# A recurrent attention with router and two feed-forward layers on one core: whole-chunk loads, products in halves, fillers in a bank of their own

## The chip, the core and the metric

The kernel runs on one core of a Trainium2 chip. The metric is the device time in microseconds (us) of one execution. Five engines work from queues of their own, each strictly in its written order: TensorE (PE, with its weight loads shown as PEld), VectorE (DVE), ScalarE (ACT), GpSimd (POOL) and SyncE (SP), which issues most transfers. They meet at semaphores.

## What is computed

The reference, cut to what matters. The shapes are B = 4, H = 8, S = 768, D = 48; N = 3072 tokens of 384 values; E = 8 experts with hidden width 1024; then a dense layer of width 2048.

```python
for t in range(S):                                   # recurrent attention, one state per (b, h)
    cur = np.einsum('bhd,bhe->bhde', u[None] * kt, vt)
    y[:, :, t] = np.einsum('bhd,bhde->bhe', rt, state + cur)
    state = wt[:, :, :, None] * state + np.einsum('bhd,bhe->bhde', kt, vt)
# the expert layer on x = y as (N, 384)
xn = x / (np.linalg.norm(x, axis=-1, keepdims=True) + 1e-06)
en = expert_emb / (np.linalg.norm(expert_emb, axis=-1, keepdims=True) + 1e-06)
logits = xn @ en.T / tau
expert_idx = np.argmax(logits, axis=1)               # each token goes to one expert
out[mask] = gate_w[mask, None] * (np.maximum(x[mask] @ w1[e], 0.0) @ w2[e])
# the dense layer
h = x @ w_in
out = (h * np.tanh(softplus(h))) @ w_out
```

## The kernel before

The program has three stages: the attention with the router woven into it, the expert layer, and the dense layer. The change touches the first alone, and that stage ends when the last token rows have been sent to their experts.

**Chunks.** The 768 steps are cut into NCH = 12 chunks of C = 64 steps. A chunk holds all 32 pairs of batch and head: two heads lie one above the other on the 128 partitions (48 rows used of each 64), 16 such pairs along the free axis. For each chunk, `load` and `load_v` bring w, r, k and v. Before, each comes in two transfers of 48 (v: 64) partitions, through `copy_in`, which views the rows as 12 (v: 8) groups. `scaled` makes running products of w from both ends with two VectorE scans (PRE, SUF) and from them RH = r·PRE (POOL) and KH = k·SUF (VectorE).

**Products on TensorE.** All are fp32, and the profile counts two records for one such product. For a chunk: `keys` (transposes of KH), `bonus` (RK = r·k from POOL as the weights, the columns of u as the moving side: the term of a step with itself), `dots` (KH by RH inside the chunk), `sums` (into the state) and `fn` in `outputs` (RH by the state, L617, then the matrix `at` by v, L622). The router handles two tiles of 128 tokens per chunk (`Router.tile`): `turn` (transposes of x), `logits` (x by the expert embeddings), then ScalarE copies; after 6, 6, 6, 4 and 2 tiles `decide` ranks the tokens of that group (norm by `inv_norm`, arg max, ranks on TensorE) and `send` scatters the tiles' rows to the table xs in DRAM by POOL's indirect transfers.

**The matrix `at`** is made of the bonus spread on a diagonal (h = 0 by eight ScalarE activations, L548; h = 1 by one POOL product, L558, as ON_POOL says for every chunk) and the dots copied into its upper part by VectorE (L565).

**Fillers.** Ahead of each chunk's bonus TensorE runs FILL = 2 bf16 products of 128x512 whose result nobody reads (L541); they write the PSUM bank that the bonus then uses. After the attention 60 more products of 128x256 (`ahead`, L981) follow.

**What sets the order.** The scheduler of the framework is off. Every step is registered with `plan.add`; the list ORDER names the steps in the order of issue, and BANKS names for each temporary result one of seven PSUM banks. An engine takes its own steps of that list in that order. Transfers issued by SP use eight completion semaphores in turn, so one waits for the eighth before it.

**At the end of the stage** the last scatter must land before SP loads the first expert's rows (`load_rows`, L957); ScalarE and VectorE scale them, TensorE turns them (L1007), and the first expert product (L1021) starts.

## Time and profile before

| what | us |
|---|---|
| median of 3 runs (lowest, highest) | 815.65 (815.36, 817.05) |
| the profiled execution, its own time | 821.62 |
| its span, first to last instruction | 819.9 |
| first work of TensorE | 11.9 |
| end of the last chunk's outputs on TensorE | 152.2 |
| first expert product | 179.25 |

The profile gives, for each engine, busy time by groups of instructions and by stretches of the span, the waits with the engine that ended them, and a timeline in which a row stands for consecutive instructions of one kind. A weight load and the product that uses it overlap, so a group's busy time divided by its count is a pace and not the length of one. The rows used are in a section of their own below.

### The profile page before, as it was taken

The numbers are of one execution on the slowest core, as the hardware profiler recorded it, in microseconds if no ns is written. First come the engines' busy times: TensorE is split into PE (matmuls) and PEld (weight loads), VectorE is DVE, ScalarE is ACT, GpSimd is POOL, SyncE is SP. The second block draws the span as 40 slices with busy tenths as digits, with TensorE's granted clock in tenths as the row PEclk, the third lists the DMA queues.
The fourth block names the chain that finished last, engine by engine and source line by source line (L and its number), as shares of the span: only waits on it lengthen the run. The fifth ranks groups of instructions, "written<-read, shape, count | busy, mean of one in ns | idle before, by whom it ended". The sixth has DMA issues, their size and how long they took to land. (4 is left out here: it accounts for less than half of the span.)

```text
span 819.9 us, 17379 instructions
## 1 busy us (share of the span) xinstructions
PE 777.7 (95%) x6464; PEld 715.9 (87%) x6464; DVE 638.3 (78%) x954; ACT 484.6 (59%) x1049; POOL 431.7 (53%) x391
## 2 busy tenths in 40 slices
PE   3998999789999999999999999999999999999995
PEld 3897987768999999989989999999999999999994
DVE  9895885558988898898878778877876776876773
ACT  4584665436566656647556566666656665665653
POOL 9695866337778787767433353334334334335331
PEclk9998899779999999999999999999999999999998
DMA  6765453167777777775200010000001001001001
GB/s 183 196 195 162 150 158 125 60 187 186 199 175 180 196 185 181 193 199 177 59 1 1 0 40 1 1 20 20 1 1 40 1 0 39 1 2 39 0 1 44
DMA packets 61357, 73.79 MB, mean 90 GB/s; under 512 B 8966, under 2 KB 51886, under 8 KB 61262
## 3 DMA queue, kind: packets, MB, share of 16 engines
q1 hardware_dynamic: 57422, 63.11, 28.4%
q0 software_dynamic: 3840, 9.47, 3.2%
q8 instruction: 53, 0.87, 0.5%
q14 instruction: 42, 0.34, 0.1%
HBM read 61.86 MB, written 10.69 MB: 88 GB/s over the span
## 5 line engine op out<-in xcount | busy, mean ns | idle before, releaser
L1151 POOL TENSOR_TENSOR t<-t,t 128x512 f32<-128x512 f32 x94 | 121.9, 1299 | 237.2 <-ACT t L1147 231.7
L1160 DVE TENSOR_TENSOR gl<-t,gh 128x512 fp32r<-128x512 f32 (+1 forms) x97 | 114.1, 1176 | 74.5 <-ACT gh L1157 74.2
L1144 ACT ACTIVATE t<-t,two 128x512 f32<-128x512 f32 (+1 forms) x97 | 69.9, 720 | 118.4 <-DVE t L1141 118.4
L872 PE MATMUL acc<-woh,gl 128*128 128x384 f32 x384 | 129.6, 338 | 0.1
L870 PE MATMUL acc<-woh,gh 128*128 128x384 f32 x384 | 129.3, 337 | 0.0
L871 PE MATMUL acc<-wol,gh 128*128 128x384 f32 x384 | 129.0, 336 | 0.0
L949 POOL TENSOR_TENSOR w0l<-r,w0h 128x384 fp32r<-128x384 f32 x63 | 68.4, 1086 | 60.2 <-ACT w0h L948 52.3
L865 PE MATMUL ph<-xl,wih 128*128 128x512 f32 x240 | 95.0, 396 | 0.0
L864 PE MATMUL ph<-xh,wil 128*128 128x512 f32 x240 | 94.8, 395 | 0.0
L863 PE MATMUL ph<-xh,wih 128*128 128x512 f32 x240 | 93.3, 389 | 0.0
L870 PEld LDWEIGHTS acc<-woh,gh 128*128 128x128 f32 x384 | 72.2, 188 | 4.2
L949 POOL TENSOR_TENSOR w1l<-r,w1h 128x384 fp32r<-128x384 f32 x63 | 74.6, 1184 | 1.9 <-ACT w1h L948 1.5
L871 PEld LDWEIGHTS acc<-wol,gh 128*128 128x128 f32 x384 | 72.1, 188 | 4.0
L872 PEld LDWEIGHTS acc<-woh,gl 128*128 128x128 f32 x384 | 72.0, 188 | 0.4 <-DVE gl L1160 0.4
L865 PE MATMUL acc<-hl,w1h 128*128 128x428 f32 (+7 forms) x192 | 67.2, 350 | 3.6 <-DVE hl L1030 3.4
L1154 DVE TENSOR_TENSOR t<-t,ph 128x512 f32<-128x512 f32 (+1 forms) x97 | 64.8, 668 | 5.8 <-POOL t L1151 5.7
L863 PE MATMUL acc<-hh,w1h 128*128 128x428 f32 (+7 forms) x192 | 67.6, 352 | 1.8 <-DVE yT L1045 1.8
L1157 ACT CAST gh<-t 128x512 fp32r<-128x512 f32 (+1 forms) x97 | 58.8, 606 | 16.5 <-DVE t L1154 14.3
L1141 DVE SCALAR_TENSOR_TENSOR t<-t 128x512 f32<-128x512 f32 (+1 forms) x97 | 66.2, 683 | 2.1 <-ACT t L1137 2.1
L1134 DVE TENSOR_SCALAR t<-ph 128x512 f32<-128x512 f32 (+1 forms) x97 | 65.3, 674 | 2.4 <-PE ph L865 2.2
L864 PE MATMUL acc<-hh,w1l 128*128 128x428 f32 (+7 forms) x192 | 66.1, 344 | 0.0
L863 PE MATMUL ph<-xh,w0h 128*128 128x420 f32 (+7 forms) x189 | 65.2, 345 | 0.0
(221 smaller groups left out, 1855.9 us busy)
## 6 DMA issues: line engine op xcount, KB each, us to landing
r<-in_moe_w SPq DMA_DIRECT2D x128, 192.0 KB
d<-in_moe_w_in SPq DMA_DIRECT2D x16, 384.0 KB
d<-in_moe_w_out SPq DMA_DIRECT2D x16, 384.0 KB
r<-in_r_t SPq DMA_DIRECT2D x24, 192.0 KB
k<-in_k_t SPq DMA_DIRECT2D x24, 192.0 KB
v<-in_v_t SPq DMA_DIRECT2D x24, 192.0 KB
w<-in_w_t SPq DMA_DIRECT2D x22, 198.0 KB
xs<-zs SPq DMA_DIRECT2D x1, 1203.1 KB
```

The lines of the kernel that those rows point to most:

```text
L863: mm(out, lhsT=wh, rhs=xh, start=start, stop=False)
L864: mm(out, lhsT=wl, rhs=xh, start=False, stop=False)
L865: mm(out, lhsT=wh, rhs=xl, start=False, stop=stop)
L870: mm(out, lhsT=ah, rhs=bh, start=start, stop=False)
L871: mm(out, lhsT=ah, rhs=bl, start=False, stop=False)
L872: mm(out, lhsT=al, rhs=bh, start=False, stop=stop)
L949: (eng or nc.gpsimd).tensor_tensor(lo, r, f32(hi), op=ALU.subtract)
L1134: nc.vector.tensor_scalar(tile_of(i, "t0", mt, bufs=3)[:, q], S[i]["ph"][:, q], 20.0, None, op0=ALU.min)
L1141: nc.vector.scalar_tensor_tensor(t0, t0, 2.0, t0, op0=ALU.add, op1=ALU.mult)
L1144: nc.scalar.activation(tile_of(i, "t1", mt)[:, q], S[i]["t0"][:, q], AF.Ln, bias=g.two)
L1151: (nc.gpsimd if i < TI - 2 else nc.vector).tensor_tensor(t0, t0, S[i]["t1"][:, q], op=ALU.mult)
L1160: nc.vector.tensor_tensor(tile_of(i, "gl", ghl, F32R)[:, q], S[i]["t0"][:, q], f32(S[i]["gh"][:, q]), op=ALU.subtract)
```

## The change

- **Loads.** The two heads' 48 rows now lie next to one another (partitions 16 to 111: LEAD = 16, HEADS), so w, r and k of a chunk come in one transfer of 96 partitions each; v in two of 64, without the view in groups. The first load of w keeps its 128 partitions. The initial rows of the table xs are written by eight transfers of 100 rows instead of one of 8 x 100.
- **Bonus and logits in halves.** Each product with 128 weight columns becomes two with 64, whose results go to the lower and the upper half of the PSUM partitions.
- **Fillers.** None ahead of the bonus any more; FILL = 37 single fillers (L637) are steps of their own, in the last PSUM bank, and six banks are left for BANKS.
- **`at`.** ON_POOL holds for even chunks alone; in the six odd ones ScalarE makes h = 1 as well.
- **Sums of squares.** In `decide`, VectorE first copies them to PSUM (`twin`), and the later product reads the copy.
- **u.** Its two small copies into `ub` go from VectorE to ScalarE.
- **A new ORDER and a new BANKS**, with changed costs in the planner's steps (bonus 0.9 + 0.44 becomes 1.7).

```diff
-FILL = 2
-ON_POOL = [(s, 1) for s in range(NCH)]
+FILL = 37
+ON_POOL = [(s, 1) for s in range(0, NCH, 2)]
...
 ORDER = [
-    2, 16, 18, 6, 3, 4, 10, 0, 20, 19, 27, 9, 8, 11, 5, 7, 31, 12, 17, 32, 25, 29, 37, 38,
+    2, 20, 27, 10, 18, 29, 0, 11, 3, 7, 6, 1, 8, 4, 16, 5, 19, 31, 32, 12, 154, 17, 109, 9,
...
+    if twin is not None:
+        add("dve", STEP, lambda: v.tensor_copy(s2, ss), [src], [ks])
...
-            ("dve", lambda: v.tensor_tensor(t, ss, r, op=ALU.mult), [src, kr], kt),
+            ("dve", lambda: v.tensor_tensor(t, s2, r, op=ALU.mult), [ks, kr], kt),
...
-                nc.tensor.matmul(lg(), lhsT=xT[:, c], rhs=g.enT[:, c], start=c == 0, stop=c == KC - 1)
+                for q in COLS:
+                    nc.tensor.matmul(lg()[q], lhsT=xT[:, c, q], rhs=g.enT[:, c], start=c == 0, stop=c == KC - 1)
...
-    def copy_in(x, rows, e=SPREAD):
-        b = rows.shape[0] // e
-        nc.sync.dma_start(x, rows.rearrange("(b e) n -> e b n", b=b))
...
+            q = HEADS if s else slice(0, 128)
+            add("sp", BW * 0.3, lambda: nc.sync.dma_start(W[s % NW][q], g.w_t[s, q]), [], [("w", s % NW)], wake=1.3)
...
-        for h in range(2):
-            out = dst[s % NR][64 * h:64 * h + D].rearrange("p n t -> p (n t)")
-            add("sp", BW * 0.2, lambda out=out, h=h: copy_in(out, src[s, h]), [], [(nm, s % NR)], wake=1.3)
+        add("sp", BW * 0.3, lambda: nc.sync.dma_start(dst[s % NR][HEADS].rearrange("p n t -> p (n t)"), src[s]), [], [(nm, s % NR)], wake=1.3)
...
-            for _ in range(FILL):
-                pe.matmul(plan.view(kb, 512), lhsT=g.ident.bitcast(BF16)[:, :128], rhs=g.wide, start=True, stop=True)
             for jp in range(2 * NP):
-                pe.matmul(plan.view(kb, 2 * NP, 2)[:, jp], lhsT=RK[:, 2 * jp:2 * jp + 2].rearrange("p b t -> p (b t)"), rhs=ub[:, jp // 2],
-                          start=True, stop=True)
+                for q in range(2):
+                    pe.matmul(plan.view(kb, 2 * NP, 2)[ROW[q], jp], lhsT=RK[:, 2 * jp + q], rhs=ub[:, jp // 2], start=True, stop=True)
...
-            add("sp", BW * 1.2, lambda: nc.sync.dma_start(
-                g.xs[:, :].rearrange("(e n) d -> n e d", e=E)[CAP - REST:CAP], zs.rearrange("p (o d) -> p o d", o=1).to_broadcast([REST, E, XW])),
-                ["zs"], ["slots"])
+            for e in range(E):
+                add("sp", 0.8, lambda e=e: nc.sync.dma_start(g.xs[e * N + CAP - REST:e * N + CAP, :], zs), ["zs"], ["slots"])
...
+    idle = g.banks[-1]
+
+    def fill():
+        pe.matmul(idle, lhsT=g.ident.bitcast(BF16)[:, :128], rhs=g.wide, start=True, stop=True)
...
+    for _ in range(FILL):
+        add("pe", 0.22, fill, ["wide", "ident"], ["fill"], recs=2)
```

How the new table and the other parts stand in the queues, at three places.

TensorE, the bonus of the eighth chunk (`wide` and `ident` are the operands of a filler, `ub` and `rk` those of the bonus, `enT` and `r_xT` those of the logits). Before:

```order
L321 MATMUL bank_86<-enT,r_xT_97 128x8 x3
L317 MATMUL bank_82<-ident,x 128x128 x3
L541 LDWEIGHTS ident
L541 MATMUL bank_80<-wide,ident 128x512
L541 LDWEIGHTS ident
L541 MATMUL bank_80<-wide,ident 128x512
L543 MATMUL bank_80<-ub_130,rk_140 128x2 x8
L588 MATMUL bank_84<-v_119,kb_117 64x48
```

and after the change, the ninth bonus of the queue:

```order
L322 MATMUL bank_84<-ident,x 128x128 x3
L573 MATMUL bank_85<-ident,kh_110 128x128 x4
L637 LDWEIGHTS ident
L637 MATMUL bank_86<-wide,ident 128x512
L327 MATMUL bank_80<-enT,r_xT_97 64x8 x6
L327 MATMUL bank_84<-enT,r_xT_96 64x8 x6
L541 MATMUL bank_83<-ub_130,rk_140 64x2 x16
L585 MATMUL bank_85<-v_119,kb_117 64x48
```

Two fillers in the bonus' own bank have gone, one stands elsewhere in bank 86; eight products of the bonus are sixteen, three of the logits six. Of the 37 fillers 16 stand ahead of the last chunk's outputs, 7 between those and the ranks of the fourth group, 3 between the ranks of the last two groups, 11 after them.

TensorE, behind the last chunk's outputs. Before:

```order
L622 MATMUL bank_83<-v_121,at_116 64x2x48 x2
L321 MATMUL bank_82<-enT,r_xT_95 128x8 x3
L321 MATMUL bank_81<-enT,r_xT_96 128x8 x3
L321 MATMUL bank_85<-enT,r_xT_97 128x8 x3
L317 MATMUL bank_81<-ident,x 128x128 x3
L317 MATMUL bank_82<-ident,x 128x128 x3
L321 MATMUL bank_81<-enT,r_xT_96 128x8 x3
L321 MATMUL bank_82<-enT,r_xT_97 128x8 x3
L361 LDWEIGHTS tri_149
```

and after the change:

```order
L327 MATMUL bank_84<-enT,r_xT_97 64x8 x6
L637 LDWEIGHTS ident
L637 MATMUL bank_86<-wide,ident 128x512
L637 LDWEIGHTS ident
L637 MATMUL bank_86<-wide,ident 128x512
L322 MATMUL bank_83<-ident,x 128x128 x3
L637 LDWEIGHTS ident
L637 MATMUL bank_86<-wide,ident 128x512
L322 MATMUL bank_85<-ident,x 128x128 x3
L327 MATMUL bank_80<-enT,r_xT_95 64x8 x6
```

Five logits and two transposes stood there before; now it is four logits and three transposes, with seven fillers between them.

ScalarE, the eighth chunk, an odd one counted from 0 (`at_116` is the matrix of the odd chunks). Before:

```order
L327 COPY r_lg_105<-bank_83 128x8
L554 COPY bon_129<-bank_80 128x16
L324 COPY r_xT_96<-bank_82 128x384
L548 ACTIVATE at_116<-same_132,bon_129 128x64 x8
L632 COPY x<-bank_83 128x2x4x48
L327 COPY r_lg_105<-bank_82 128x8
```

and after the change:

```order
L333 COPY r_lg_105<-bank_84 128x8
L545 ACTIVATE at_116<-same_132,bon_129 128x64 x16
L576 COPY kb_118<-bank_80 128x512
L384 ACTIVATE r_lg_105<-r_lg_105 128x6x8
L505 ACTIVATE junk_145,viol_126<-w_135,bias_127 128x1024
```

Sixteen activations stand in a row where there were eight; a copy that empties a PSUM bank follows behind them. It is so in two of the six odd chunks; in the other four the second eight stand apart from the first.

## Rows read from the trace of the kernel before

**Rows 1.** The page: the span, and TensorE's busy time, share and instructions.

```profile
span 819.9 us, 17379 instructions
PE 777.7 (95%) x6464; PEld 715.9 (87%) x6464; DVE 638.3 (78%) x954; ACT 484.6 (59%) x1049; POOL 431.7 (53%) x391
```

**Rows 2.** Busy time by stage: stretch, length, engines (instructions), granted clock, DMA share, GB/s.

```profile
11.90:152.20 140.30, 133.75 (x3090) 120.54 (x3090) 107.55 (x173) 86.22 (x291) 96.67 (x91) 0.95 0.53 157
152.20:179.20 27.00, 18.98 (x125) 15.38 (x123) 10.66 (x62) 7.65 (x26) 11.37 (x12) 0.69 0.49 160
179.20:819.90 640.70, 624.97 (x3252) 580.00 (x3252) 510.15 (x701) 388.00 (x732) 312.85 (x268) 0.99 0.26 71
```

**Rows 3.** TensorE's waits from 11.9 to 152.2: total us, times, longest.

```profile
PE bank L622 <- issue: 2.7, 1, 2.7
...
PE bank L536 <- ACT enT L255: 0.3, 1, 0.3
```

**Rows 4.** Groups of TensorE from 10 to 165: count, busy, mean ns, idle before.

```profile
L543 PE MATMUL bank<-ub,rk 128*128 128x2 f32 x192 | 25.5, 264 | 0.7 <-POOL rk L551 0.7
...
L321 PE MATMUL bank<-enT,r_xT 128*128 128x8 f32 x144 | 19.8, 262 | 0.9 <-ACT r_xT L324 0.9
...
L541 PE MATMUL bank<-wide,ident 128*128 128x512 bf16 x24 | 8.1, 421 | 0.0
```

**Rows 5.** Timeline: start, length, engine, line, operation; runs at full clock.

```profile
56.77 1.35 PEld L622 LDWEIGHTS bank<-v,at 128*64 128x64 f32 x32
56.77 1.54 PE L622 MATMUL bank<-v,at 128*64 128x96 f32 x32
...
74.15 1.97 PEld L543 LDWEIGHTS bank<-ub,rk 128*128 128x128 f32 x16
74.36 1.84 PE L543 MATMUL bank<-ub,rk 128*128 128x2 f32 x16
...
76.06 0.81 PE L321 MATMUL bank<-enT,r_xT 128*128 128x8 f32 x6
```

**Rows 6.** Busy time in two stretches of the attention, columns as in rows 2.

```profile
30.00:60.00 30.00, 29.73 (x788) 27.55 (x779) 28.38 (x37) 24.05 (x76) 24.66 (x24) 1.00 0.70 186
...
70.40:98.00 27.60, 27.26 (x550) 25.21 (x548) 17.27 (x22) 15.10 (x50) 18.59 (x17) 0.76 0.42 128
```

**Rows 7.** Groups of VectorE, ScalarE and POOL around `at`, 11.9 to 152.2.

```profile
L565 DVE COPY_PREDICATED at<-after,bank 128x512 f32<-128x512 int32 x24 | 16.5, 722 | 17.3 <-PE bank L536 17.2
...
L548 ACT ACTIVATE at<-same,bon 128x64 f32<-128x64 f32 x96 | 24.2, 339 | 0.2
...
L558 POOL TENSOR_TENSOR at<-same,bon 128x512 f32<-128x512 f32 x12 | 12.7, 1056 | 12.5 <-ACT bon L554 12.5
```

**Rows 8.** Timeline: the start of TensorE's work.

```profile
10.03 0.68 DVE L518 TENSOR_TENSOR kh<-k,suf 128x512 f32<-128x512 f32 x1
...
11.89 1.97 PE L576 MATMUL bank<-ident,kh 128*128 128x128 f32 x8 [11.89 <-POOL ident masks.py:199]
```

**Rows 9.** Timeline: behind the last chunk's outputs.

```profile
156.62 2.93 PE L321 MATMUL bank<-enT,r_xT 128*128 128x8 f32 x12 [0.86 <-ACT r_xT L324]
...
172.27 1.94 SPq L957 DMA_DIRECT2D xr<-xs  x4
...
179.25 1.44 PE L1021 MATMUL ph<-xh,w0h 128*128 128x428 f32 x3 [0.51 <-ACT xh L1009]
```

**Rows 10.** SP's transfers from 20 to 50: packets, MB, share of 16 engines.

```profile
q1 hardware_dynamic: 1811, 5.76, 68.3%
```

**Rows 11.** Timeline: the transfer to xs, and a load behind it.

```profile
56.05 0.47 SPq L679 DMA_DIRECT2D xs<-zs  x1
...
70.43 1.19 POOL L518 TENSOR_TENSOR rh<-r,pre 128x512 f32<-128x512 f32 x1 [1.40 <-DMA r<-in_r_t]
```

**Rows 12.** Timeline: 64 records of the dots at either clock.

```profile
62.19 1.16 PE L536 MATMUL bank<-rh,kh 64*64 64x64 f32 x64
...
72.17 1.82 PE L536 MATMUL bank<-rh,kh 64*64 64x64 f32 x64
```

More of the change, by code (lines that the diff above doesn't have):

```diff
@@ L46 @@
 BW = 5.0
-SPREAD = 12
 SLACK, LATE_S, LATE_F, LATE_O, LATE_A = 0.02, 18.0, 0.0, 20.0, 40.0
 COLS = [slice(0, 64), slice(64, 128)]
+LEAD = DP - D
+HEADS = slice(LEAD, LEAD + 2 * D)
 REST = 100
@@ L255, in setup_experts, with inv_norm @@
     add("act", 0.1, lambda: nc.scalar.copy(g.enT, plan.view(k, KC, E)), [k], ["enT"])
-def inv_norm(g, plan, ss, r, t, out, nm, src, dst):
+def inv_norm(g, plan, ss, r, t, out, nm, src, dst, twin=None):
     v, a, add = g.nc.vector, g.nc.scalar, plan.add
@@ L495, in load_v @@
             out = V[s % NV][ROW[q], q].rearrange("p a j h d -> p (a j h d)")
-            add("sp", BW * 0.2, lambda out=out, q=q: copy_in(out, g.v_t[s, q], 8), [], [("v", s % NV)], wake=1.3)
+            add("sp", BW * 0.2, lambda out=out, q=q: nc.sync.dma_start(out, g.v_t[s, q]), [], [("v", s % NV)], wake=1.3)
     def tokens(x, at):
@@ L552, in scores @@
                 [("r", nr), ("k", nr)], [("bon", i)])
-        add("pe", 0.9 + 0.22 * FILL, bonus, [("bon", 0), ("bon", 1), "ub", "ident", "wide"], [kb], recs=32 + 2 * FILL)
+        add("pe", 1.7, bonus, [("bon", 0), ("bon", 1), "ub"], [kb], recs=64)
         add("act", 0.2, lambda: a.copy(BON[:, s], plan.view(kb, 2 * NP, 2)), [kb], [("own b", s)])
@@ L659, in attention @@
     for h in range(2):
-        add("dve", 0.1, lambda h=h: v.tensor_copy(ub[ROW[h], :, h], uc[ROW[h]]), ["uc"], ["ub"])
+        add("act", 0.1, lambda h=h: a.copy(ub[ROW[h], :, h], uc[ROW[h]]), ["uc"], ["ub"])
     for n in range(NV):
```

29 lines of the change are left out of this document (9 added, 20 removed), and 65 rows, old and new, of the table ORDER.

## The prediction

> **What bounds the kernel now.** Over the whole span TensorE is busy 95% and no other engine over 78% [rows 1], so I read the busy times by stage first. From 179.2 us on, TensorE is busy for 624.97 of 640.70 us [rows 2], in stages whose code the change leaves alone, so I keep these 640.7 us as they are. Open are the 179.2 us ahead of them. From TensorE's first work at 11.9 to the end of the last chunk's outputs at 152.2 it is busy for 133.75 of 140.30 us, VectorE for 107.55, POOL for 96.67, ScalarE for 86.22 [rows 2]. A busy PE may still be waiting inside a record, so the waits come next: the longest in that stretch is one of 2.7 us that nothing shown explains, and waits on a bank being emptied are 0.3 us [rows 3]. Seen from the other side, VectorE stood for 17.3 us before it could copy the dots, nearly all of it for TensorE [rows 7]. TensorE is the bound there, with one exception: from 30 to 60 us VectorE is busy for 28.38 of 30 us as well [rows 6]. The last 27 us are a chain (logits, ranks, six scatters, the load of the rows, the first product), in which TensorE runs at a granted clock of 0.69 [rows 2].
>
> What costs TensorE its time: the bonus, 192 records in 25.5 us; the logits, 144 in 19.8 us; the 24 fillers, 8.1 us [rows 4]. The change aims at these three.
>
> **The sum.** I make it as a difference against the profiled execution (821.62 us, span 819.9) and take the difference off the median of 815.65; the profiled one is 6.0 us longer than that, and I know no reason why the difference should be another there.
>
> *Bonus in halves.* At the full clock a chunk's 16 records take 1.84 us [rows 5], 115 ns each. The nearest row to a load of 128 x 64 with results in alternating halves is L622: 32 such records in 1.54 us, 48 ns each, and their loads alone in 1.35 us, 42 ns [rows 5]. The new bonus has 32 records, so 1.54 us: 0.30 us less, times 12 chunks, 3.6 us less. Ends: nothing, if two half loads take as long as a whole one; 5.9 us less at 42 ns. L622 streams 96 columns and the bonus 2, so I see no reason for more than 48 ns.
>
> *Logits in halves.* A tile's 6 records take 0.81 us [rows 5]. Twelve at 48 ns are 0.58 us, 0.23 less. Some 20 of the 24 tiles lie ahead of the last outputs: 4.6 us less; ends nothing, and 6.0 (0.51 us a tile, 42 ns).
>
> *Fillers.* The old ones stand in TensorE's queue ahead of each bonus, in a stretch where it hardly idles: 8.1 us on the path [rows 4]. Of the new ones 16 stand there; at the same 0.34 us each (8.1 by 24) 5.4 us. So 2.7 us less; the others are counted below. Ends 2 to 4.
>
> Together 10.9 us less of TensorE's work ahead of 152.2.
>
> *What the neighbours take back.* In 30 to 60 us VectorE leaves only 1.6 us [rows 6], while 30 of 140.3 parts of the saving would be 2.3 us: 0.7 us are lost. ScalarE gets 48 activations more, half of its present 96, which cost 24.2 us: 12.1 us [rows 7]; POOL loses six products of 1.056 us. ScalarE's total of 98 us would still fit in 130. A late `at` first uses up VectorE's wait for the dots, 17.3 us [rows 7], and costs nothing until that is gone. But ScalarE also empties the banks, of which six are left for seven, and the waits of 0.3 us [rows 3] were measured with seven. Ends: nothing, and the whole 12.1 us. I take 3 us, a quarter, since the wait that covers it is longer than the work. Together 3.7 us back.
>
> *Start.* VectorE ends the first half of KH at 10.71, but TensorE waits for the identity matrix until 11.89 [rows 8]. The new table builds that matrix earlier on POOL. At most 1.2 us; I take 0.6, since the second half costs VectorE another 0.68 us [rows 8].
>
> *End of the stage.* Two tiles' logits take 2.93 us there at the low clock [rows 9]; in halves and at the full clock 2 x 0.58 = 1.16 us, 1.8 less. Against that stand a third transposition and seven fillers (2.4 us) in places where TensorE otherwise waits for ScalarE and VectorE. If they fill waits and hold the clock it is 1.8 us less, if they are in the way 0.6 more; I take 1.0 less. The 11 fillers behind the last ranks run beside the scatters and the row loads, which at 172.27 [rows 9] still have 7 us to the first product; I cost them at nothing while the clock is high; at half of it they would take 7.5 us and eat that cover.
>
> *Loads.* SP's transfers keep 0.68 of the 16 engines busy [rows 10]; whole loads may spread wider and land sooner. But no TensorE wait on a load shows up in [rows 3]. The waits near the one big transfer to xs (2.7 us in [rows 3], 1.4 us of POOL in [rows 11]) may go, and eight smaller ones among the chunk loads may bring others: zero, from 4 less to 3 more.
>
> *The rest at nothing.* The copies of the squares (five, a few columns) lie in VectorE's 33 idle us, and its two copies of u move to an engine with 54 idle us [rows 2].
>
> Sum: -10.9 + 3.7 - 0.6 - 1.0 = -8.8, so 815.65 - 8.8 = **806.9 us**.
>
> **The rivals.**
>
> *Halves buy nothing (0.19).* For: nothing in the trace shows a load of 64 columns with a moving side of 2. Against: L622's 42 ns are a third of the 123 ns (1.97 us by 16) that a load of 128 columns takes, not half [rows 5]. Then bonus and logits give 0, the end 0.6, and with less saved less is taken back (1): -2.7 - 0.6 - 0.6 + 1 = -2.9, 812.8 us. A rule would have it so: the Trainium skill, TensorE: Matmul & The Clock Gate, section "LDWEIGHTS (loading the stationary operand)", lets the time of a load go by its columns, and section "The mechanism" lets a load overlap running products only where the row group differs, which halves over all 128 rows do not. By that rule the time would be this rival's; L622's loads, also over all rows, come out faster than it says.
>
> *ScalarE or the banks become the bound (0.14).* All 12.1 us come onto the path instead of 3: -8.8 + 9.1 = +0.3, about 815.5 us. For: in two odd chunks sixteen activations (5.4 us at 339 ns) stand ahead of a bank's copy. Against: the 17.3 us [rows 7].
>
> *The clock falls (0.17), the one on the slow side.* From 70.4 to 98 us the granted clock was 0.76 [rows 6], so some 13 us at 1.2 GHz instead of 2.4, although TensorE counts as busy for 27.26 of 27.60. The dots then took 1.82 us instead of 1.16 [rows 12]: each such us loses 0.36. The change takes 512-column products out of every chunk and leaves those with 2 and 8 columns. It gives back the 8.8 us from 24 us more at the low clock on; with 36 more it loses 13, and the time is **819.9 us**. For: fewer wide products, and a TensorE with less work has more gaps. Against: 16 fillers are left, and from 30 to 60 us the clock stayed at 1.00 [rows 6] with little more.
>
> **How the numbers follow.** My forecast has 0.50, between 801 and 811. The range takes in the halves' rival and ScalarE's, and down to the sum of the good ends: halves at 42 ns (3.7 more), nothing back (3.7), no waits for loads, would be near 797, of which I leave the tip out: 799 to 816.5. About 0.2% (1.6 us) is what a measurement here can tell from no change. Faster by more: 0.50 + 0.18 of the halves' rival + 0.07 of ScalarE's + 0.01 = 0.76. Within: 0.01 + 0.06 + 0.01 = 0.08. Slower: 0.01 of ScalarE's and 0.15 of the clock's, 0.16.
>
> **What would show it.** In the changed kernel's profile: a bonus of 32 records in 1.5 us and a tile's logits of 12 in 0.6 (1.8 and 0.8 mean that the halves buy nothing); the last outputs' end near 144.5 instead of 152.2 and the first expert product near 170.5 instead of 179.25; 640 us behind it as before. New waits of TensorE on ScalarE copies would speak for the banks; a mean clock from 12 to 150 below 0.9 for the clock. What makes the forecast wrong most easily is the 3 us for the neighbours: it is a guess between 0 and 12.

## The result, and the profile of the changed kernel

| | before | changed |
|---|---|---|
| median of 16 runs (lowest, highest), us | 815.5 (811.9, 822.1) | 821.9 (818.0, 825.7) |
| ratio, 95% interval | 1 | 1.0085 (1.0063 to 1.0107) |
| the profiled execution: own time, span | 821.62, 819.9 | 823.47, 821.7 |

The changed kernel is slower by 7 us by the ratio (6.4 us by the medians), where 8.8 us faster was forecast; 821.9 lies outside the range. Ratios leave out executions more than 1.5% above the fastest of the same kernel, so they need not equal the ratio of the medians. (The two profiled executions differ by 1.85 us only, since that of before was 6 us above its median. So the traces show where work and waits moved, and not the whole loss.)

The page and the busy time by stage of the changed kernel (columns as in [rows 1, 2]):

```profile
span 821.7 us, 18054 instructions
...
PE 765.6 (93%) x6813; PEld 698.4 (85%) x6813; DVE 642.5 (78%) x957; ACT 495.5 (60%) x1099; POOL 426.3 (52%) x385
...
10.90:154.50 143.60, 120.36 (x3397) 104.53 (x3398) 111.99 (x175) 96.77 (x341) 93.90 (x89) 0.90 0.57 152
154.50:181.60 27.10, 19.78 (x166) 13.56 (x165) 12.14 (x66) 7.83 (x26) 9.56 (x10) 0.83 0.48 157
181.60:821.70 640.10, 625.39 (x3252) 580.28 (x3252) 509.14 (x700) 388.35 (x731) 312.91 (x268) 0.99 0.27 71
```

Against [rows 2]: the 640 us behind the first expert product are as they were, and so are the 27 us of the chain ahead of it. The whole difference of the two traces lies in the attention, which begins 1.0 us earlier and ends 2.3 us later. In it TensorE is busy for 13.4 us less (133.75 before, 120.36 now) and idle for 16.7 us more (6.55 before, 23.24 now). So the work went away as planned, and more than all of it came back as idle time. The clock is worse too: 0.90 where it was 0.95, that is (1 - clock) x 2 x length, 28.7 us at 1.2 GHz instead of 14.0.

What TensorE waits for now (us in total, times, longest; "issue" is idle time in which it waited for nothing that the profile names; before, one wait of 2.7 us was the longest [rows 3]):

```profile
PE bank L585 <- DVE at L562: 6.1, 1, 6.1
PE bank L619 <- issue: 4.3, 3, 2.9
PE bank L541 <- POOL rk L548: 3.6, 1, 3.6
PE bank L535 <- issue: 2.0, 3, 1.1
PE bank L541 <- issue: 1.7, 2, 1.3
PE bank L541 <- DVE state L595: 1.4, 1, 1.4
```

The halves themselves did more than forecast. Groups of TensorE from 10 to 165 us (against [rows 4]), and from the timeline (start and length in us, engine, line, operation) a chunk's bonus and a tile's logits at the full clock (against [rows 5]):

```profile
L541 PE MATMUL bank<-ub,rk 128*64 128x2 f32 x384 | 14.3, 203 | 6.8 <-POOL rk L548 3.6 <-issue 1.7 <-DVE state L595 1.4
...
L637 PE MATMUL bank<-wide,ident 128*128 128x512 bf16 x32 | 12.2, 445 | 0.0
L327 PE MATMUL bank<-enT,r_xT 128*64 128x8 f32 x288 | 11.9, 207 | 0.1
```

```profile
22.97 1.10 PE L541 MATMUL bank<-ub,rk 128*64 128x2 f32 x32
...
45.55 0.52 PE L327 MATMUL bank<-enT,r_xT 128*64 128x8 f32 x12
```

32 records in 1.10 us are 34 ns each (48 were forecast), 12 in 0.52 are 43 ns. Bonus and logits together fell from 45.3 to 26.2 us.

The longest new wait, from the timeline (VectorE's and POOL's rows name the step; the brackets tell the idle time ahead and who ended it):

```profile
97.24 1.01 POOL L392 DMA_INDIRECT xs<-x,desti  x1 [0.16 <-issue]
97.34 1.54 PE L619 MATMUL bank<-v,at 128*64 128x96 f32 x32
97.59 7.17 DVE L517 TENSOR_TENSOR kh<-k,suf 128x512 f32<-128x512 f32 x2
...
98.28 0.84 POOL L600 TENSOR_TENSOR state<-sum,own 128x384 f32<-128x384 f32 x1
...
99.08 1.26 POOL L548 TENSOR_TENSOR rk<-r,k 128x512 f32<-128x512 f32 x1
...
100.30 2.30 POOL L517 TENSOR_TENSOR rh<-r,pre 128x512 f32<-128x512 f32 x2
102.57 1.04 POOL L555 TENSOR_TENSOR at<-same,bon 128x512 f32<-128x512 f32 x1
...
104.85 1.26 DVE L562 COPY_PREDICATED at<-after,bank 128x512 f32<-128x512 int32 x2
...
105.56 2.13 PE L585 MATMUL bank<-v,kb 64*64 64x48 f32 x64 [6.14 <-DVE at L562]
```

Two products of VectorE that take 0.68 us each otherwise [rows 8] last 7.17 us; the first alone has 6.57. It ends when POOL's row of five products ends. Behind it waits the copy of the dots, and behind that a bank, so TensorE stands still for 6.14 us, and the clock falls after it: granted clocks of 0.73 in this stretch and of 0.79 in the one behind the idle start.

```profile
30.00:60.00 30.00, 28.75 (x769) 25.76 (x772) 25.56 (x34) 22.97 (x81) 19.95 (x18) 0.79 0.64 185
...
95.00:120.00 25.00, 15.02 (x388) 13.32 (x389) 19.66 (x24) 7.27 (x24) 13.81 (x14) 0.73 0.49 121
```

This was the first suspect. When the hold was taken out, its 6 us did not come back (last group below).

### The profile page after: what moved, and what is told of

Read it like the earlier page. It is cut to its first block, busy times and chain, and to the rows that moved or that the text cites. A ratio compares the mean times of both kernels' runs of the same rounds, so it can differ in the third digit from the quotient of the medians.

```text
span 821.7 us, 18054 instructions
## 1 busy us (share of the span) xinstructions
PE 765.6 (93%) x6813; PEld 698.4 (85%) x6813; DVE 642.5 (78%) x957; ACT 495.5 (60%) x1099; POOL 426.3 (52%) x385
```

## The experiments

Series of runs differ (the kernel before took 814 us in one and 827 in another, and 815 and 827 on a chip of the same number), so everything is compared as a ratio to the kernel before in the same series on the same chip. "Wide loads" are the single transfers of 96 partitions, "split loads" the two of 48. "Old order" means ORDER and BANKS of before; where a step exists once in place of twice it takes the first one's place.

| kernel | ratio | 95% interval |
|---|---|---|
| halves alone (e1) | 0.9893 | 0.9841 to 0.9946 |
| e1 and the rest, without wide loads (e5) | 0.9927 | 0.9881 to 0.9973 |
| e1 without fillers (e11) | 0.9930 | 0.9884 to 0.9976 |
| e1 on the new rows of the tiles (e14) | 0.9939 | 0.9899 to 0.9978 |
| e1, both loads at the first one's place (e16) | 0.9967 | 0.9928 to 1.0006 |
| halves and wide loads, later place (e15) | 0.9997 | 0.9953 to 1.0040 |
| halves and wide loads (e6) | 1.0009 | 0.9971 to 1.0048 |
| all parts, old order (e2) | 1.0047 | 1.0002 to 1.0091 |
| wide loads alone (e4) | 1.0058 | 1.0023 to 1.0094 |
| halves and wide loads in 12 groups (e10) | 1.0074 | 1.0029 to 1.0119 |
| changed, without fillers (e8) | 1.0072 | 1.0042 to 1.0102 |
| **the changed kernel** | 1.0085 | 1.0063 to 1.0107 |
| changed, with the long wait taken out (e12) | 1.0104 | 1.0046 to 1.0162 |
| changed, at full width (e3) | 1.0153 | 1.0077 to 1.0229 |
| changed, with split loads (e7) | 1.0213 | 1.0151 to 1.0275 |

### The parts, one by one

**e1_halves_old_table.** The kernel before with this alone:

```diff
-                pe.matmul(plan.view(kb, 2 * NP, 2)[:, jp], lhsT=RK[:, 2 * jp:2 * jp + 2].rearrange("p b t -> p (b t)"), rhs=ub[:, jp // 2],
+                for q in range(2):
+                    pe.matmul(plan.view(kb, 2 * NP, 2)[ROW[q], jp], lhsT=RK[:, 2 * jp + q], rhs=ub[:, jp // 2], start=True, stop=True)
...
-                nc.tensor.matmul(lg(), lhsT=xT[:, c], rhs=g.enT[:, c], start=c == 0, stop=c == KC - 1)
+                for q in COLS:
+                    nc.tensor.matmul(lg()[q], lhsT=xT[:, c, q], rhs=g.enT[:, c], start=c == 0, stop=c == KC - 1)
```

> The kernel before with one part alone: bonus and logits in halves of 64 columns; loads, fillers, engines, banks and the table as they were. The new trace has 32 bonus products in 1.10 us where 16 took 1.84, and 12 pairs of logits products in 0.50 us where 6 of full width took 0.81 for a tile: 12 x 0.74 + 24 x 0.31 = 16 us less work of TensorE. Theory A (the saving is real, the new table gives it back in waits): the stage was 95% TensorE, so at least half of it shows, 803 to 809 against 815.5. Theory B (the neighbours' chains take all of it, whatever the table): 813 to 817. Theory C (the wide loads lose it): as A here, since the loads are the old ones.

0.9893, by the ratio 8.7 us less. In its timeline (start and length in us, engine, line) the last outputs and the first expert product are

```profile
142.47 1.54 PE L626 MATMUL bank<-v,at 128*64 128x96 f32 x32
...
168.70 1.44 PE L1025 MATMUL ph<-xh,w0h 128*128 128x428 f32 x3 [0.51 <-ACT xh L1013]
```

so the outputs end at 144.0 and the expert layer starts at 168.7: the forecast had put these marks at 144.5 and 170.5 for the whole change. The busy time up to there (columns as in [rows 2]):

```profile
11.90:144.00 132.10, 119.94 (x3393) 103.47 (x3403) 109.63 (x173) 86.25 (x291) 95.49 (x91) 0.95 0.58 167
```

Theory B falls. This kernel is faster than both others.

**e2_all_old_table.** All parts but the separate fillers and the table:

```diff
-FILL = 37
+FILL = 2
...
+            for _ in range(FILL):
+                pe.matmul(plan.view(kb, 512), lhsT=g.ident.bitcast(BF16)[:, :128], rhs=g.wide, start=True, stop=True)
```

> All parts of the change but its table and its separate fillers: 96-partition loads, halves, eight zero rows' transfers, twin copies, every second mask product on ScalarE; the order and the seven banks of before (where two loads stood, the one load stands at the first one's place), two fillers inside each bonus as before. Theory A (the table): near the kernel with the halves alone, 802 to 812. Theory B: 812 to 818. Theory C (the loads): 818 to 824, as the changed kernel.

1.0047, by the ratio some 819 us where the changed kernel takes 821.9: at the lower end of Theory C's band, and far from the 802 to 812 of Theory A, which blamed the table alone and falls as well. Table and separate fillers together come to 0.4%, and by the intervals to anything from nothing to 0.9%.

**e3_new_table_full_width.** The changed kernel with the hunk of e1 undone.

```diff
-                for q in range(2):
-                    pe.matmul(plan.view(kb, 2 * NP, 2)[ROW[q], jp], lhsT=RK[:, 2 * jp + q], rhs=ub[:, jp // 2], start=True, stop=True)
+                pe.matmul(plan.view(kb, 2 * NP, 2)[:, jp], lhsT=RK[:, 2 * jp:2 * jp + 2].rearrange("p b t -> p (b t)"), rhs=ub[:, jp // 2],
...
```

> The changed kernel with bonus and logits at full width again (one product of 128 columns where there are two of 64); all else, the new table too, as changed. Between 10.9 and 154.5 us TensorE is idle for 23.2 us in the changed kernel. Theory A: TensorE's 16 us more fall partly into these idle stretches, but the stretch from 115 to 154.5 has none, so 4 to 12 us slower than the changed kernel, 826 to 834. Theory B (the neighbours' chains set the end): within 2 us of it, 820 to 824. Theory C as A.

1.0153, by the ratio 0.7% above the changed kernel (the intervals overlap at their ends): as far as that can tell, the halves are worth about as much under the new order as under the old.

**e4_loads_old_table.** The kernel before with the wide loads alone:

```diff
-        for h in range(2):
-            out = dst[s % NR][64 * h:64 * h + D].rearrange("p n t -> p (n t)")
-            add("sp", BW * 0.2, lambda out=out, h=h: copy_in(out, src[s, h]), [], [(nm, s % NR)], wake=1.3)
+        add("sp", BW * 0.3, lambda: nc.sync.dma_start(dst[s % NR][HEADS].rearrange("p n t -> p (n t)"), src[s]), [], [(nm, s % NR)], wake=1.3)
...
```

> The kernel before with one part alone: loads of 96 partitions from plain rows (one of r, k and w for a chunk where there were two, v in whole rows), each at the place of the first of the two; the rest as before. Theories A and B: the loads are not what ends late, 813 to 818. Theory C: with the 16 DMA engines at a share of 1.0 in place of 0.7 while they load, whatever else uses them (scatters, code) waits longer, 819 to 824.

1.0058 (about 4.7 us): slower, in the band of Theory C. Its trace has hardly any new idle time on TensorE, but a lower clock in the middle of the attention. The kernel before, then this one:

```profile
60.00:95.00 35.00, 31.94 (x684) 29.40 (x687) 22.83 (x40) 17.23 (x60) 21.96 (x21) 0.84 0.50 155
95.00:120.00 25.00, 24.57 (x650) 22.22 (x642) 21.68 (x32) 16.74 (x60) 18.52 (x17) 0.95 0.62 178
```

```profile
60.00:95.00 35.00, 33.91 (x662) 31.38 (x664) 22.18 (x40) 17.63 (x61) 19.30 (x19) 0.76 0.47 122
95.00:120.00 25.00, 22.50 (x462) 21.15 (x463) 17.73 (x25) 11.20 (x42) 16.24 (x16) 0.80 0.77 190
```

Why the clock is lower is not shown. (The edit also lets the load of the second chunk's w go without waiting for the first chunk's r and k. TensorE's first work comes at 11.9 us with either form of load in the old order, so this does not show at the start.)

### Which of the other parts cost it

**e5_halves_rest_old_table.** e2 with the hunk of e4 undone (split loads); eight transfers of zeros, twin copies, every second `at` on ScalarE stay.

```diff
+    def copy_in(x, rows, e=SPREAD):
+        b = rows.shape[0] // e
+        nc.sync.dma_start(x, rows.rearrange("(b e) n -> e b n", b=b))
...
+            add("sp", BW * 0.2, lambda out=out, h=h: copy_in(out, src[s, h]), [], [(nm, s % NR)], wake=1.3)
```

> The kernel with all parts in the old order (821.2 beside 814.2 of before) less the wide loads: halves, eight zero rows' transfers, twin copies, every second mask product on ScalarE, old split loads, old order and banks. Adding up what was measured apart (halves -8.7, wide loads +4.7, all together +3.8 by the ratios, so +7.8 for the rest): 814 beside 814.2. Theory D (VectorE's product of two SBUF tiles gets its turn only when GpSimd pauses, and it was the wide loads that took GpSimd's waits for r away; in the kernel with all parts one product was held 6.2 us for that): without the wide loads no product is held beyond 3 us and the time is 805 to 810. Theory E (the mask products on ScalarE or the zero rows cost it by themselves): 814 to 818.

0.9927: the rest costs nothing that can be told from e1 (0.3% more, with intervals that overlap), so the guess of +7.8 us for it falls. From this kernel to e2 the wide loads alone are added, and they cost 1.2%.

**e6_halves_loads_old_table.** e1 and the hunk of e4.

```diff
+        add("sp", BW * 0.3, lambda: nc.sync.dma_start(dst[s % NR][HEADS].rearrange("p n t -> p (n t)"), src[s]), [], [(nm, s % NR)], wake=1.3)
...
+                for q in range(2):
+                    pe.matmul(plan.view(kb, 2 * NP, 2)[ROW[q], jp], lhsT=RK[:, 2 * jp + q], rhs=ub[:, jp // 2], start=True, stop=True)
```

> Halves and wide loads, nothing else of the change, old order and banks. Added up: -8.7 + 4.7 = -4, 808 to 812 beside 814.2. Theory D: the mask products are all on GpSimd, which waits for the bonus copies before 7 of them, so it still pauses; no product held beyond 3 us, and the time is the sum. If halves and wide loads alone already leave GpSimd without pauses, a product is held 5 us or more and the time is 814 to 820.

1.0009: the wide loads take the whole gain of the halves, 1.2% from e1. In its trace no product is held longer than 3.08 us, so a long hold is not needed for that. But this trace shows little of the loss: its execution took 810.5 us, 4.6 us below the kernel's median, and that of e1 took 810.7 us.

**e7_after_split_loads.** The changed kernel with the hunk of e4 undone.

```diff
-        add("sp", BW * 0.3, lambda: nc.sync.dma_start(dst[s % NR][HEADS].rearrange("p n t -> p (n t)"), src[s]), [], [(nm, s % NR)], wake=1.3)
+        for h in range(2):
+            out = dst[s % NR][64 * h:64 * h + D].rearrange("p n t -> p (n t)")
+            add("sp", BW * 0.2, lambda out=out, h=h: copy_in(out, src[s, h]), [], [(nm, s % NR)], wake=1.3)
...
```

> The changed kernel with the loads of before (two of 48 partitions in 12 groups where there is one of 96, v in 8 groups), each pair at the place of the one; new order, banks and fillers. If the wide loads cost what they cost in the old order: 4 to 5 us faster than the changed kernel, 815 to 819 beside 814 to 815.5 of before. If the new order is made for them (loads land earlier, as it counts on): the same or slower, 821 to 828.

1.0213: worse, not better. With the old loads TensorE waits 5.8 us ahead of its first bonus, 3.7 us for KH and 2.9 us for v, which looks like an order that counts on loads landing early. So what wide loads cost within the new order is not shown, and an undone part tells something only in an order that wasn't written for it.

### What about the wide loads it is

**e10_wide_loads_12_groups.** e6 with the loads laid out in groups:

```diff
-        add("sp", BW * 0.3, lambda: nc.sync.dma_start(dst[s % NR][HEADS].rearrange("p n t -> p (n t)"), src[s]), [], [(nm, s % NR)], wake=1.3)
+        add("sp", BW * 0.3, lambda: copy_in(dst[s % NR][HEADS].rearrange("p n t -> p (n t)"), src[s]), [], [(nm, s % NR)], wake=1.3)
```

> Halves and wide loads in the old order, as the kernel with both that gave 815.0, but each transfer is laid out in 12 groups of 8 rows (v in 8 groups), as the loads of before were in 12 groups of 4; still one transfer of 96 partitions where there were two. Theory F (the plain transfer fills all 16 DMA engines, share 1.0 where it was 0.7, and whatever else needs one waits: TensorE's idle time put down to issue is 10.7 us in the two old-order kernels with halves and plain wide loads, 5.9 and 8.5 in the two with split loads): back near the halves alone, 806 to 811. Theory G (that one transfer stands where two stood, at the first one's place): 813 to 817.

1.0074, some 821 us beside 815.4: above both bands. Theory F falls. From 30 to 60 us the DMA engines are as free as with split loads (a share of 0.69; e1 0.70, e6 0.77), and the gain doesn't come back.

**e14_split_loads_new_rows**, **e15_wide_loads_second_place**, **e16_split_loads_first_place.** e1 with the tile's rows moved; e6 with the load at the second one's place in ORDER; e1 with the second load right behind the first.

```diff
-            out = dst[s % NR][64 * h:64 * h + D].rearrange("p n t -> p (n t)")
+            out = dst[s % NR][LEAD + D * h:LEAD + D * h + D].rearrange("p n t -> p (n t)")
...
```

> Halves in the old order with split loads of 48 partitions in 12 groups of 4 at their old places; only the rows of the tiles are the changed kernel's (16 to 111 in place of 0 to 47 and 64 to 111). Beside before on the same chip, halves alone gave 0.989 and halves with wide loads 1.001 (plain) and 1.007 (12 groups). If the rows cost it: 1.000 to 1.008. If it is that one transfer stands for two, or where it stands: 0.985 to 0.994.

> Halves and plain wide loads in the old order, with the one transfer at the place of the second of the two that it replaces, not the first. If the early place costs it (a transfer of 384 KB starts where one of 192 KB did and delays the ones behind it): 0.986 to 0.996. If the place does not matter: 0.998 to 1.007. If a later place is worse, since both halves now start later: above 1.007.

> Halves in the old order with the old split loads and rows, but the second of each pair brought up to the first one's place. If the place is what costs in the wide loads: 0.998 to 1.007. If not: 0.985 to 0.994, as the halves alone.

0.9939, 0.9997 and 0.9967. The rows aren't it (inside the band of the halves), the later place brings nothing back, and the early place alone may cost 0.3 to 0.7% or nothing (between its two bands). The five kernels with halves and split loads lie between 0.989 and 0.997, mean 0.993; the four old-order ones with halves and wide loads between 1.000 and 1.007, mean 1.003. Wide loads cost 1.0% (0.5 to 1.5% by the spread of the nine), about 8 us. Between e16 and e6, which differ in the form of the loads, the rows and the point noted at e4, it is 0.4% with intervals that overlap, so how the 1.0% divides between the form and the place isn't settled.

The product KH that was held in the changed kernel is held in three of these nine as well, in e2, e10 and e16 (shortest, median and longest of 24, ns):

```profile
L515 DVE TENSOR_TENSOR kh<-k,suf x24: 627/682/6207, 10.0 to 140.6; 128x512 f32<-128x512 f32 x24
L519 DVE TENSOR_TENSOR kh<-k,suf x24: 627/684/6658, 10.0 to 144.0; 128x512 f32<-128x512 f32 x24
L522 DVE TENSOR_TENSOR kh<-k,suf x24: 615/680/6543, 10.0 to 139.7; 128x512 f32<-128x512 f32 x24
```

In the other six none takes over 3.08 us. The three are the slowest of their groups: e16 lies 0.4% above the other four with split loads, e2 and e10 0.6% above the other two with wide ones. So such a hold may cost about that much where it occurs; with one trace for each kernel this is not shown. Without the three the wide loads still cost 0.8% (0.992 and 1.000).

In the same nine traces TensorE's idle time put down to "issue" (nothing that the profile shows held it) splits the same way: 5.9 to 8.5 us from 12 to 152 us with split loads, 9.6 to 10.7 with wide ones. Rows of that cause among TensorE's waits (us in total, times, longest), first of e1, then of e6:

```profile
PE bank L626 <- issue: 2.8, 3, 1.3
```

```profile
PE bank L585 <- issue: 3.9, 2, 2.3
PE bank L325 <- issue: 2.5, 1, 2.5
```

That suggested that TensorE's code comes in later behind a wide transfer. The traces bear out the first half of it. They have a DMA queue of kind "instruction", q8, that moves packets of 16 KB, and their number goes with TensorE's instructions: 24 packets from 12 to 152 us before, where TensorE ran about 3090 products and as many loads, and 27 in e1, where it was about 3470, some 257 instructions a packet in both. Of the 48 gaps of 0.5 us or more that the nine traces put to "issue", 45 end 1.2 to 1.8 us after such a packet has landed. The 2.5 us of e6 above, from the timeline, and the queues in the 1.3 us in which its packet was under way (packets, MB, share of 16 engines):

```profile
55.22 0.41 PE L325 MATMUL bank<-enT,r_xT 128*64 128x8 f32 x8 [2.54 <-issue]
```

```profile
q1 hardware_dynamic: 88, 0.25, 96.5%
q8 instruction: 1, 0.02, 6.1%
```

The 2.7 us of the kernel before [rows 3] end 1.4 us after such a packet too. These waits come to 2.7 to 8.1 us with split loads (mean 5.0) and 7.2 to 10.7 us with wide ones (mean 8.9).

**e18_code_under_loads.** The kernel before and, behind the attention, eight stretches of this under each form of load:

```diff
+    def code(gate, n=24):
+        for i in range(n):
+            for jp in range(2 * NP):
+                for q in range(2):
+                    last = (i, jp, q) == (n - 1, 2 * NP - 1, 1)
+                    pe.matmul(g.banks[i % 2].rearrange("p (a b) -> p a b", b=2)[ROW[q], jp], lhsT=(gate if last else RK)[:, 2 * jp + q], rhs=ub[:, jp // 2],
+                              start=True, stop=True)
```

> The kernel before with work added behind the attention stage: eight stretches in which TensorE runs 768 products of 64 columns in a straight line with no wait, while the DMA queue brings in 12 times 384 KB from r in one form: none, split (two transfers of 48 partitions in 12 groups), wide (one plain transfer of 96), groups (one of 96 in 12 groups), none, wide, split, groups. Its time adds nothing to the comparison. Theory H (TensorE's code is fetched later behind wide transfers): idle time put down to issue under 1 us without loads, 1 to 3 us a stretch under split ones, 2 us or more above that under wide ones and groups. Rival (loads do not delay it, or all forms alike): the three forms within 1 us of each other.

A stretch is 384 products, which the profile counts as 768 records. In all eight stretches together TensorE waited 0.6 us for "issue", so by the stated bounds the rival. But both waits (0.20 and 0.43 us) fall under plain wide loads, and both end 1.5 us after a packet of q8 has landed. The packets themselves start up to 6.9 us apart without loads, up to 9.9 and 8.1 us apart in the two stretches under split loads, 11.5 and 11.0 under wide ones, and 9.6 and 10.2 under wide ones in groups. So loads do hold up the code, and plain wide ones the longest. Busy time by stretch, without loads, with split and with wide ones (these two with a DMA share of 0.45 and 0.44):

```profile
168.00:208.00 40.00, 40.00 (x754) 40.00 (x754) 1.34 (x14) 0.00 (x0) 3.89 (x4) 0.50 0.08 27
209.00:249.00 40.00, 40.00 (x756) 40.00 (x754) 0.00 (x0) 0.00 (x0) 0.00 (x0) 0.50 0.45 120
250.00:290.00 40.00, 39.80 (x746) 39.72 (x744) 0.00 (x0) 0.00 (x0) 0.00 (x0) 0.50 0.44 120
```

It cost next to nothing here: the whole ran at 1.2 GHz, at some 19 records per us, where in the attention 64 records of the sums or dots follow one another in 1.2 to 1.5 us and use their code up faster. By what the wide loads cost their 1% stays open all the same: the longer waits for code are at most half of it by their means (3.9 of 8 us), e6's trace has 5 us more of them than e1's and took no longer, and e4 has less idle time of this kind than before (4.6 us against 5.5) and a lower clock.

### The fillers

**e11_halves_no_fillers.** e1 with

```diff
-FILL = 2
+FILL = 0
```

> Halves in the old order (807.9) without the two filler products of 512 columns at the head of each bonus: 24 products that took 8.1 us of TensorE before. If TensorE's work sets the end: 800 to 805. If the fillers lie in waits that come anyway, or keep the clock up: 806 to 812, with as much or more time at the lower clock (13.6 us between 10 and 152 us in the kernel with them).

**e8_after_no_fillers.** The changed kernel without the last lines of its `attention`:

```diff
-    for _ in range(FILL):
-        add("pe", 0.22, fill, ["wide", "ident"], ["fill"], recs=2)
```

> The changed kernel without its 37 separate filler products, order and banks as they are: 12.2 us less of TensorE's busy time in the stage. If they lie in waits that come anyway (TensorE idles 23.2 us in the stage): 1.004 to 1.013 of before, as the changed kernel's 1.0085. If they delay the work behind them: 0.996 to 1.003. If they hold the clock up: above 1.013, with more than the 27.4 us at the lower clock in the stage.

0.9930 beside e1's 0.9893, and 1.0072 beside 1.0085: fillers of 8 and of 12 us can be left out without a difference that these runs can tell, in either order. That they lie in waits that come anyway fits the new order, where the clock from 12 to 152 us is 0.94 without them and 0.90 with them. In the old order it is 0.91 without and 0.95 with, some 11 us more at 1.2 GHz, so there they may also pay for themselves by the clock; one trace each doesn't settle it.

### The product that is held

**e9_port_rows.** Behind the attention stage of the kernel before, five times on scratch tiles (0, 1, 3, 6, 6 products behind the first; the last time with one operand in PSUM):

```diff
+        p.tensor_tensor(RK[:, half], R[0][:, half], K[0][:, half], op=ALU.mult)
+        if kind == "two":
+            v.tensor_tensor(R[1][:, half], RK[:, half], K[0][:, half], op=ALU.mult)
...
+        for _ in range(n):
+            p.tensor_tensor(junk[:, half], R[0][:, half], K[0][:, half], op=ALU.mult)
```

> The kernel before, with work on scratch tiles added behind the attention stage: five rows on GpSimd, each a product of 128x512 and then 0, 1, 3, 6 and 6 more of them without a wait between; VectorE is asked for one product of 128x512 when the first of the row is done. In the first four rows both its operands are in SBUF, in the fifth one is in a PSUM bank. Its time adds nothing to the comparison. One product on VectorE alone takes 0.68 us, one on GpSimd 1.2 to 1.27. Theory D (a two-SBUF product waits until GpSimd pauses, however many products that is): about 0.7, 1.9, 4.4 and 8.0 us, and 0.6 to 0.7 for the fifth. Rival (the port changes hands after each instruction): 0.7, then 1.9 at most, in every row.

0.69, 1.73, 1.73, 1.73 us, and 0.69 with one operand in PSUM: held by one product of POOL, however many follow. The rival held here.

**e13_rows_by_kind.** The same, with another instruction of POOL under VectorE's request:

```diff
+    for kind in ("product", "mask", "state", "memset", "scatter", "scatter"):
+        row(kind)
+    row("product", more=2)
+    row("scatter", more=2)
```

> The kernel before with work on scratch tiles behind the attention stage: on GpSimd a product, then one instruction of a kind (product, mask product with both operands repeated, state product with one, memset, scatter, scatter), then five products without a wait; VectorE asks for its product of two SBUF tiles when the first is done, so under the instruction of that kind. Two more rows with two such products on VectorE, under a product and under a scatter. Its time adds nothing to the comparison. Theory D2: about 1.7 us under a product, a state product or memset, and 6 to 8 us (until the row ends) under a scatter, perhaps under a mask product too (in the kernel with all parts one asked for under a mask product was held 6.2 us). Rival (held by the one running instruction, whatever it is): 0.7 to 2.0 in every row.

1.75 us under a product, 1.52 a mask product, 1.31 a state product, 0.69 a memset and the scatters (there VectorE had begun 0.1 us before the scatter). Two such products in a row took 3.40 us under products, and 1.42 us under a scatter, where the second was asked for while it ran. So one instruction again.

**e17_rows_asked_late.** POOL's row of the changed kernel, VectorE asking later:

```diff
+    for kind, *sizes in (("product", 384), ("mask", 32), ("mask", 384), ("scatter", 128), ("scatter", 384), ("scatter", 512, 256)):
+        row(kind, *sizes)
```

> The kernel before with work on scratch tiles behind the attention stage: on GpSimd a product, one instruction of a kind, then the row of the changed kernel at 98.28 us (state product, a product of r and k, two of r and pre, mask product); VectorE asks for the product of k and suf behind copies of 32 to 768 elements, so 0.1 to 1 us after the instruction of that kind began: product 384; mask 32, 384; scatter 128, 384, 768. Its time adds nothing to the comparison. If a product asked for under a scatter, or at some moment of a mask product, is held through the row: 6 to 7 us in those rows. If not: under 2 us in all, and what held it in the changed kernel stays open.

Five of the six asks were through in 0.68 to 1.42 us. The first was not:

```profile
184.83 1.27 POOL L695 TENSOR_TENSOR junk<-r,k 128x512 f32<-128x512 f32 x1
184.92 0.56 DVE L705 COPY bank<-rk 128x384 f32<-128x384 f32 x1 [4.73 <-POOL rk L695]
185.39 6.54 DVE L706 TENSOR_TENSOR kh<-k,suf 128x512 f32<-128x512 f32 x1
...
186.05 0.84 POOL L715 TENSOR_TENSOR state<-sum,own 128x384 f32<-128x384 f32 x1
186.85 1.25 POOL L695 TENSOR_TENSOR junk<-r,k 128x512 f32<-128x512 f32 x1
...
190.34 1.04 POOL L699 TENSOR_TENSOR at<-same,bon 128x512 f32<-128x512 f32 x1
```

Asked for at 185.39, it gets its turn after the mask product, when POOL's row is through. So a product of VectorE with both operands in SBUF can be held through a whole row; it was asked for 0.56 us into a product here, 0.35 us into a scatter in the changed kernel. Other requests at such moments passed. What decides it stays open.

**e12_after_row_repaired.** The changed kernel, POOL's steps around 97 to 104 us in another order (POOL's own steps, picked out of the list; 226 and 227 are the scatters, 501 the mask product):

```diff
- 568, 226, 421, 569, 566, 564, 501, 227
+ 568, 421, 569, 501, 566, 564, 226, 227
```

> The changed kernel with two steps of GpSimd's order moved: the scatter at 97.24 us goes behind the row that follows it, to the next scatter, and the mask product at 102.57 goes ahead of the two rh products at 100.30. In the changed kernel VectorE's product kh was asked for at 97.59, under that scatter, and held until the row of five ended, 6.57 us; TensorE then idles 6.14 us and the clock is at its lower level for 13.7 us. Theory D2 (a product asked for under a scatter is held through the row behind it): no kh above 2 us here, TensorE idles 3 us or less at this place, and 816 to 820 against 821.9. Rival (the end is set elsewhere, the stall is cover): 820 to 824 although the stall is gone.

No KH product is above 1.76 us, and the wait on VectorE at this place is 0.19 us (it was 6.14). Yet the time is 1.0104: nothing gained, and by the intervals 0.4% at most of the 0.7% that the 6 us would be. In its trace TensorE has another loss instead, under the last row of scatters:

```profile
151.47 0.79 PE L614 MATMUL bank<-state,rh 64*64 64x48 f32 x37
...
152.65 0.35 PE L614 MATMUL bank<-state,rh 64*64 64x48 f32 x3 [0.39 <-issue]
152.69 0.97 POOL L392 DMA_INDIRECT xs<-x,desti  x1 [0.30 <-issue]
...
154.14 0.46 PE L614 MATMUL bank<-state,rh 64*64 64x48 f32 x4 [0.41 <-issue]
...
158.46 0.33 PE L614 MATMUL bank<-state,rh 64*64 64x48 f32 x1 [0.48 <-issue]
```

64 records that take 1.15 us elsewhere take 7.3 here, some six of these us while the scatters run. Such gaps of 0.2 to 0.5 us, within 2.2 us of the start of a scatter, do not need the repaired order: e10, e11, e14 and e16, like e12 from series in which the kernel before took 823 us or more, have eight or more each, the kernel before has five, and the changed kernel, e5, e6 and e8 have none. What brings them is not shown. As they may have cost e12 what the repair gave, this run does not show what the hold was worth; the three kernels with a hold above would put it at 3 to 5 us.

## Why the prediction was wrong

**Bonus and logits in halves: the net is right, by two errors that offset each other.** 8.2 us less of TensorE's work ahead of the last outputs were forecast, of which VectorE was to take back 0.7 us. In e1's trace TensorE has 13.8 us less work there (119.9 us for 133.75), and 5.6 us of that come back as waits, so its outputs end 8.2 us earlier (144.0 for 152.2). By the ratio the halves alone gave 8.7 us less (4.4 to 13.0), their four near relations 0.3 to 0.7% less. So the pace was mis-sized one way, and the reading that TensorE is the bound and nearly all of a saving shows was wrong the other way. The pace was under the good end of the bounds for the bonus (34 ns against 42 to 48) and inside them for the logits. "Halves buy nothing" falls, and with it the rule of the Trainium skill (TensorE: Matmul & The Clock Gate, "LDWEIGHTS (loading the stationary operand)" and "The mechanism") as it was applied to it. An estimate by that rule, columns over 1.2, gives 53 ns for a load of 64; 34 ns were measured for load and product together, so here the measurement decides.

**Loads at nothing: the step that failed.** The prediction had argued that no wait on a load shows in [rows 3], and so gave zero, 4 less to 3 more. Measured in the old order: 4.7 us more alone, 8 us more beside the halves. The argument was wrong in kind: here a transfer cost time without anyone waiting for its data. In e2, e6 and e15 the waits on a load that the profile lists for VectorE, ScalarE and POOL come to 0.6 us or less, fewer than before (e10, in groups, has them again). What showed up was longer waits of TensorE for its code, and in e4 a lower clock. The row that could have warned was the 2.7 us of "issue" in [rows 3], put at nothing. How much of the 8 us goes by which way stays open.

**The fillers: mis-sized.** 2.7 us less were forecast, as if each filler lay on the path because TensorE hardly idled. Left out, in either order, they gave no difference that can be told.

**The neighbours' 3 us, "most easily wrong": no sign of the miss there.** ScalarE's 48 further activations belong to the rest of e5, which costs nothing that can be told. TensorE's waits on ScalarE, the mark of that rival, came to some 1 us, and its 815.5 us was missed as well.

**The order: not costed at all.** The sum took the new table's waits only at the start, where 0.6 us less were forecast. TensorE did start 1.0 us earlier, but then waited 3.6 us for the first bonus. From the mean of the four old-order kernels with halves and wide loads, 1.003, to the changed kernel's 1.0085 are 0.5%, some 4 us, for order, fillers and the rest together; what of it is the order's was not measured apart (e2 and the changed kernel have intervals that overlap).

**The clock's rival (0.17, 819.9 us): near in time, half right in mechanism.** It wanted 36 us more at 1.2 GHz; there were 14.7 more, worth 5 us at its 0.36. In this trace it is a part of the loss, behind the new idle stretches, and not its whole; e8, with a clock of 0.94 in its trace, is hardly faster.

The sum by what was measured: -5.6 (halves, the mean of five kernels at 0.993) + 8.2 (wide loads) + 4.3 (order and the rest) = +6.9 us, the 0.85% of the result. The last term is what the others leave, so it closes by construction; and the wide loads' 8.2 us are those of the old order, carried over to the new one without a run that shows them there.

## What to carry to other kernels

Bring parts of a change in one by one, each in the order of the kernel before: a part that gains can hide one that loses as much. A transfer for which nobody waited was not free here, so when loads are merged, look also at TensorE's idle time without a named cause, at the queue that brings its code and at its clock, not only at waits on the data. And a long wait that a trace shows is worth what the time says when it is gone: here nothing came back, though another loss may have hidden it.

## What the runs showed of the hardware beyond that

- Products with 64 weight columns, their results in alternating halves of the rows, came at 34 ns a record, load included, where those with 128 columns came at 115 [rows 5], both with 2 moving columns at the full clock: less than a third.
- By the counts above TensorE's code comes in packets of 16 KB by a DMA queue of its own, and loads of data delay them: in e18 they start at most 6.9 us apart without loads and up to 11.5 us apart under wide ones. In the attention TensorE stood still until 1.2 to 1.8 us after such a packet had landed, for up to 3.0 us at a time (e2).
- A product of VectorE with two SBUF operands was held by one running product of POOL (1.73 us for 0.69) in most cases, and through a whole row of POOL's instructions in some: 6.57 us in the changed kernel, 6.54 in e17, 6.2 to 6.7 in e2, e10 and e16. The Trainium skill, SBUF — State Buffer, "SBUF: two separate sides", has the shared ports taken "for the whole instruction"; the one-instruction cases agree, the long ones go beyond it.
- TensorE that ran nothing but products of two columns without a pause was granted 0.50 of its clock, 1.2 GHz, in each of eight stretches of 40 us, although busy for 39.57 to 40.00 us of each (e18).
